# Reordering the opening of a fused linear-attention and SwiGLU kernel: half of nd, x and q transposes, and the k phi of the next batch

## Chip, cores, metric

One core of a Trainium2 chip. The metric is the device time of one execution in microseconds (us), median of a kernel's runs. All timed runs named here are in the fast state, but for the single run of e4, whose state is unknown. A ratio is the mean time of one kernel's fast runs over the mean of the other's in the same rounds, so it is not quite the ratio of the medians quoted beside it.

## The reference, cut to what matters

```python
# q, k, v: 8 batches x 8 heads x 576 tokens x 64
def phi(x, c, s):                       # c, s: cos and sin of the token's place
    r = np.maximum(x, 0.0)
    return np.concatenate([r * c, r * s], axis=-1)
kv  = np.einsum('bhsf,bhsd->bhfd', phi(k), v);   z = np.sum(phi(k), axis=2)
num = np.einsum('bhsf,bhfd->bhsd', phi(q), kv)
den = np.einsum('bhsf,bhf->bhs', phi(q), z)[..., None] + 1e-06
x   = num / den                         # tokens x 512
xn  = x / sqrt(mean(x * x) + 1e-6) * rms_g
g   = xn @ w_gate;  val = xn @ w_val    # 512 -> 1536
out = (silu(g) * val) @ w_out           # 1536 -> 512
```

Of the kernel before, what the change touches and what calls it, by code (L numbers as in the profile page):

```python
# [23 lines left out]
def kernel(  # L24
# [30 lines left out]
    psA = ps.tile([P, 2, 512], FP32, name="psA")  # L55
# [8 lines left out]
    V, A, G = nc.vector, nc.scalar, nc.gpsimd  # L64
# [160 lines left out]
    def q_phi(eng, b, c, part):  # L225
        o = slice(0, D) if part == 0 else slice(D, F)
        f = cos_of if part == 0 else sin_of
        if (b, c) not in qp_tiles:
            qp_tiles[(b, c)] = four.tile(
                [P, H if c < 4 else 4, F], BF16, name="qp", tag="qp" if c < 4 else "qpt"  # L230
            )
        src = view4(raw[("q", b)], c) if c < 4 else raw[("qt", b)][:, :, :]
        phi(eng, qp_tiles[(b, c)][:, :, o], src, f(c))
# [15 lines left out]
    def q_tr_pe(b, c, bank):  # L249
        t = qp_tiles[(b, c)]  # L250
        dst = bank.bitcast(BF16).rearrange("p (h s) -> p h s", s=P)
        for h in range(H if c < 4 else 4):
            nc.tensor.transpose(dst[:, h, :], t[:, h, :], ident[:, :])  # L253

    def q_tr_evac(eng, b, c, bank, heads=(0, 8)):
        h0, h1 = heads if c < 4 else (0, 4)
        dst = bank.bitcast(BF16).rearrange("p (h s) -> p h s", s=P)
        copy(eng, q_dst(b, c)[:, h0:h1, :], dst[:, h0:h1, :])

    def copy(eng, o, i):  # L260
        if eng is nc.scalar:
            nc.scalar.copy(out=o, in_=i)  # L262
        else:
            eng.tensor_copy(out=o, in_=i)  # L264
# [10 lines left out]
    def kvz_mm(b, banks, rs=(0, 4)):  # L275

        for r in range(*rs):
            for j in range(NJ):
                for c in range(2):
                    lo = 64 * c  # L280
                    nc.tensor.matmul(  # L281
                        banks[c][:, r * E : (r + 1) * E],
                        lhsT=kp_main[b][lo : lo + 64, j, r, :],
                        rhs=vvm[b % 2][lo : lo + 64, r, j, :],
                        start=(j == 0), stop=(j == NJ - 1),
                    )
# [4 lines left out]
    def kvz_copy(eng, b, c, bank, rs=(0, 4)):  # L291
        if (b, c) not in kvzs:
            kvzs[(b, c)] = three.tile([P, 4 * E], BF16, name="kvzs", tag=f"kvzs{c}")
        lo, hi = rs[0] * E, rs[1] * E
        copy(eng, kvzs[(b, c)][:, lo:hi], bank[:, lo:hi])
# [7 lines left out]
    def nd_pe(b, j, pst):  # L303

        o = headview(pst)
        for h in range(H):
            g, i = h // 4, h % 4
            if j < 4:
                nc.tensor.matmul(  # L309
                    o[:, g, i, :], lhsT=qpT[(b, 0)][:, h, j * P : (j + 1) * P],  # L310
                    rhs=kvz_of(b, h), start=True, stop=True,
                )
            else:
                for bb in (b - 1, b):
                    lo = 64 * (bb % 2)
                    nc.tensor.matmul(
                        o[lo : lo + 64, g, i, :],
                        lhsT=qpT[(bb, 1)][:, i, 64 * g : 64 * g + 64],
                        rhs=kvz_of(bb, h), start=True, stop=True,
                    )  # L320

    def nd_half(b, j, g, bank):
        o = bank[:, 0 : 4 * E].rearrange("p (h e) -> p h e", e=E)
        for i in range(4):
            nc.tensor.matmul(
                o[:, i, :], lhsT=qpT[(b, 0)][:, 4 * g + i, j * P : (j + 1) * P],
                rhs=kvz_of(b, 4 * g + i), start=True, stop=True,
            )
# [11 lines left out]
    def nd_post_half(b, j, g, bank):  # L340
        o = bank[:, 0 : 4 * E].rearrange("p (h e) -> p h e", e=E)
        xt = x_tile(b, j)
        rec = four.tile([P, 2, 4], FP32, name="rec", tag="rec")
        nc.vector.tensor_scalar(
            out=rec[:, g, :], in0=o[:, :, D], scalar1=1e-6, scalar2=None, op0=ALU.add
        )
        nc.vector.reciprocal(out=rec[:, g, :], in_=rec[:, g, :])
        nc.vector.tensor_tensor(
            out=xt[:, g * DM // 2 : (g + 1) * DM // 2].rearrange("p (h d) -> p h d", d=D),
            in0=o[:, :, 0:D],  # L350
            in1=rec[:, g, :].unsqueeze(2).to_broadcast([P, 4, D]),
            op=ALU.mult,
        )

    def nd_post(b, j, pst):
        o = headview(pst)
        xt = x_tile(b, j)
        rec = four.tile([P, 2, 4], FP32, name="rec", tag="rec")
        nc.vector.tensor_scalar(
            out=rec[:, :, :], in0=o[:, :, :, D], scalar1=1e-6, scalar2=None, op0=ALU.add  # L360
        )
        nc.vector.reciprocal(out=rec[:, :, :], in_=rec[:, :, :])
        nc.vector.tensor_tensor(  # L363
            out=xt[:, 0:DM].rearrange("p (b h d) -> p b h d", b=2, d=D),
            in0=o[:, :, :, 0:D],
            in1=rec[:, :, :].unsqueeze(3).to_broadcast([P, 2, 4, D]),
            op=ALU.mult,
        )

    def x_sq(b, j):  # L370
        xt = x_of[(b, j)]
        scr = one.tile([P, DM + 1], BF16, name="scr", tag="scr")
        ms = four.tile([P, 1], FP32, name="ms", tag="ms")
        nc.scalar.activation(  # L374
            out=scr[:, :], in_=xt[:, 0 : DM + 1], func=AF.Square,
            scale=1.0 / math.sqrt(DM), accum_out=ms[:, :],
        )
        rs = four.tile([P, 1], FP32, name="rs", tag="rs")
        nc.gpsimd.tensor_tensor(out=rs[:, :], in0=ms[:, :], in1=mhalf[:, :], op=ALU.pow)  # L379
        rs_of[(b, j)] = rs  # L380
# [82 lines left out]
    def filler(n, bank):  # L463
        for _ in range(n):
            nc.tensor.matmul(bank, lhsT=warm[:, 0:P], rhs=warm[:, :], start=True, stop=True)
# [60 lines left out]
    v_cast(V, 0, 3, 4)  # L526
    kvz_mm(0, high_banks, (2, 3))
    filler(1, idle)
    kvz_mm(0, high_banks, (3, 4))
    kvz_copy(A, 0, 0, high_banks[0], HIGH)  # L530
    kvz_copy(A, 0, 1, high_banks[1], HIGH)
    q_tr_evac(V, 0, 1, psO[0][:, :])
    nd_half(0, 0, 0, psV[0])
    nd_post_half(0, 0, 0, psV[0])
    filler(1, idle)
    nd_half(0, 0, 1, psO[1])
    nd_post_half(0, 0, 1, psO[1])
    copy(A, gb[:, :], psG[0][:, :])
    nd_pe(0, 1, psA)
    q_phi(A, 0, 2, 1)  # L540
    x_sq(0, 0)
    nd_post(0, 1, psA)
    filler(8, psV[1][:, :])
    q_phi(A, 0, 3, 1)
    q_phi(V, 0, 2, 0)
    x_sq(0, 1)
    gval_slice(768, 1152)
    gval_slice(1152, 1536)
    q_tr_pe(0, 2, psO[0][:, :])
    q_tr_evac(A, 0, 2, psO[0][:, :])  # L550
    x_norm(0, 0)
    q_phi(V, 0, 3, 0)
    filler(1, psV[1][:, :])

    def open_ffn(pair, steps, c0, c1, base=0, parts=(0, 1)):

        x = xnT[0]
        for i, n in enumerate(steps):
            for a in parts:
                w = (wg, wv)[a]  # L560
                bank = pairs[pair][a]
                lo = base + 256 * i + c0 % 256
                for t in range(NDT):
                    nc.tensor.matmul(  # L564
                        bank[:, lo : lo + c1 - c0],
                        lhsT=w[:, t, n * P : (n + 1) * P], rhs=x[:, t, c0:c1],
                        start=(t == 0), stop=(t == NDT - 1),
                    )
# [13 lines left out]

    x_tr_pe(0, 0, psG[1][:, :])
    x_tr_evac(V, 0, 0, psG[1][:, :])
    q_tr_pe(0, 3, psO[1][:, :])
    x_norm(0, 1)
    open_ffn(0, (0, 1), 0, 128)
    x_tr_pe(0, 1, psV[1][:, :])
    q_tr_evac(A, 0, 3, psO[1][:, :])
    x_tr_evac(V, 0, 1, psV[1][:, :])  # L590
    nd_pe(0, 2, psA)
    nd_post(0, 2, psA)
    x_sq(0, 2)
    wo_load(0)
    filler(1, psG[1][:, :])
    open_ffn(0, (0, 1), 128, 256)
    nd_pe(0, 3, psA)
    nd_post(0, 3, psA)
    open_ffn(1, (2, 3), 0, 256)
    open_h(0, 0, 0)  # L600
    x_norm(0, 2)
    x_sq(0, 3)
    open_ffn(2, (4, 5), 0, 256, parts=(0,))
    x_tr_pe(0, 2, psA[:, 0, :])
    x_tr_evac(A, 0, 2, psA[:, 0, :])
    open_h(1, 2, 0)
    x_norm(0, 3)
    open_ffn(0, (0, 1), 256, 384)
    open_ffn(2, (4, 5), 0, 256, parts=(1,))
    x_tr_pe(0, 3, psA[:, 1, :])  # L610
    x_tr_evac(A, 0, 3, psA[:, 1, :])
    open_h(2, 4, 0)
    open_ffn(0, (0, 1), 384, 512)
    open_h(0, 0, 1)
# [33 lines left out]


    for j in range(NJ):  # L650
        at(0, 9 + j // 5, "post", k_phi, V, 1, j, 0)
        at(0, 9 + j // 5, "post", k_phi, A, 1, j, 1)
    for c in range(2):
        at(0, 11, "post", q_phi, V, 1, c, 0)
        at(0, 11, "post", q_phi, A, 1, c, 1)


    for nb in range(2, B):
# [203 lines left out]
```

## The kernel before: what the change touches

Nine blocks of 512 tokens run one after another. Block 0 has its attention at the very start (the *opening*); all later attention work hides beside the matrix products of earlier blocks (PE is busy 263.4 of the last 268.9 us). The names: `phi` is a relu times cos and sin (see the reference); `psA`, `psG`, `psO`, `psV` are tiles in PSUM, which TensorE writes and ScalarE or VectorE copy out; `kvz` is k-z-v (phi(k) times v with a column of ones); `nd` is numerator and denominator, phi(q) times kvz, for one group of 128 tokens; `x_sq` and `x_norm` make the normed x; `x_tr_pe` transposes it on TensorE into PSUM, and `x_tr_evac` copies it to `xnT`, which the gate and value products (`open_ffn`) read. `q_phi`, `q_tr_pe` and `q_tr_evac` do the same for q. `filler` is a product of zeros that keeps TensorE going. The traces show TensorE and ScalarE keeping to program order: in the kernel before TensorE stood 0.67 us until 24.79 for the copy of x2, and the products into `psO` that stand behind it and do not need x2 came at 25.68; in e4 ScalarE stood 3.48 us for k, and the SiLU behind it came at 38.09.

```python
    kvz_mm(0, high_banks, (2, 3))
    filler(1, idle)
    kvz_mm(0, high_banks, (3, 4))
    kvz_copy(A, 0, 0, high_banks[0], HIGH)
    kvz_copy(A, 0, 1, high_banks[1], HIGH)
    q_tr_evac(V, 0, 1, psO[0][:, :])
    nd_half(0, 0, 0, psV[0])
    nd_post_half(0, 0, 0, psV[0])
    filler(1, idle)
    nd_half(0, 0, 1, psO[1])
    nd_post_half(0, 0, 1, psO[1])
    copy(A, gb[:, :], psG[0][:, :])
    nd_pe(0, 1, psA)
    q_phi(A, 0, 2, 1)
    x_sq(0, 0)
    nd_post(0, 1, psA)
    filler(8, psV[1][:, :])
    q_phi(A, 0, 3, 1)
    q_phi(V, 0, 2, 0)
    x_sq(0, 1)
    gval_slice(768, 1152)
    gval_slice(1152, 1536)
    q_tr_pe(0, 2, psO[0][:, :])
    q_tr_evac(A, 0, 2, psO[0][:, :])
    x_norm(0, 0)
    q_phi(V, 0, 3, 0)
    filler(1, psV[1][:, :])
    ...
    x_tr_pe(0, 0, psG[1][:, :])
    x_tr_evac(V, 0, 0, psG[1][:, :])
    q_tr_pe(0, 3, psO[1][:, :])
    x_norm(0, 1)
    open_ffn(0, (0, 1), 0, 128)
    x_tr_pe(0, 1, psV[1][:, :])
    q_tr_evac(A, 0, 3, psO[1][:, :])
    x_tr_evac(V, 0, 1, psV[1][:, :])
    nd_pe(0, 2, psA)
    nd_post(0, 2, psA)
    x_sq(0, 2)
    wo_load(0)
    filler(1, psG[1][:, :])
    open_ffn(0, (0, 1), 128, 256)
    nd_pe(0, 3, psA)
    nd_post(0, 3, psA)
    open_ffn(1, (2, 3), 0, 256)
    open_h(0, 0, 0)
    x_norm(0, 2)
    x_sq(0, 3)
    open_ffn(2, (4, 5), 0, 256, parts=(0,))
    x_tr_pe(0, 2, psA[:, 0, :])
    x_tr_evac(A, 0, 2, psA[:, 0, :])
    open_h(1, 2, 0)
    x_norm(0, 3)
    open_ffn(0, (0, 1), 256, 384)
    open_ffn(2, (4, 5), 0, 256, parts=(1,))
    x_tr_pe(0, 3, psA[:, 1, :])
    x_tr_evac(A, 0, 3, psA[:, 1, :])
    open_h(2, 4, 0)
    open_ffn(0, (0, 1), 384, 512)
    ...
    for j in range(NJ):                  # k and q phi of batch 1, at steps 9 to 11 of block 0
        at(0, 9 + j // 5, "post", k_phi, V, 1, j, 0)
        at(0, 9 + j // 5, "post", k_phi, A, 1, j, 1)
    for c in range(2):
        at(0, 11, "post", q_phi, V, 1, c, 0)
        at(0, 11, "post", q_phi, A, 1, c, 1)
```

Steps 0 to 5 of block 0 are done in the opening, in halves and quarters of the 512 tokens; steps 6 to 11 (`gval_step`) are full width: four 128x512 products for the gate, four for the value, then a SiLU on ScalarE and a product hT on VectorE. What is attached to a step as "post" is issued behind those.

## Time and profile before

| | before |
|---|---|
| time, median of the first 3 runs | 330.49 us (330.29 to 331.8) |
| span of the profiled run | 328.9 us |
| TensorE (PE) busy | 316.5 us, 96% |
| PE busy in the last 268.9 us | 263.4 us |
| PE idle in the first 60 us | 6.9 us |

The lines themselves stand in the prediction. How to read them: a row of the order in time gives start, duration, engine, source line, what is written from what, and in brackets how long the engine stood idle before it and what ended that. A line number can be a helper's: L411 is a transpose of x, L253 one of q, L564 the products of the opening (L561 in the kernel after), L425 the full-width gate and value products, L445 the output product, L281 the k-z-v, L208 the phi on ScalarE. The idle time in brackets is counted from the modelled end of the row before, not from its start. A DMA share over 1 is as the view gives it; I read it as full. The durations 1.01, 0.58 and 0.42 us that the prediction uses are those of the trace for a copy out of PSUM: 1024 columns on ScalarE (L262, qpT), 512 on ScalarE (L262, xnT), 512 on VectorE (L264, xnT). From 27 to 31 us the weights' queue has a DMA share of 1.24, the queue of k, q and v 0.04.

### The profile page before, as it was taken

Reading aid. Unit: us, or ns where it says so; the run is one execution under the profiler, and the core shown is the slowest. Engines: PE = TensorE matmul, PEld = TensorE weight load, DVE = VectorE, ACT = ScalarE, POOL = GpSimd, SP = SyncE. Lnnn points to the kernel's source line nnn. Section 1 sums busy time; section 2 is a strip of 40 time slices with the busy share of each in tenths; the row PEclk is TensorE's granted clock in tenths of the full one; section 3 lists DMA queues with packets and bytes.
Section 4 is the critical chain, followed back from the end, with each engine's and each line's share of the span. In section 5 each row is a group of like instructions: output and inputs, shape, how many; then the busy total and the mean of one; then the engine's idle time right before and its main releaser. Section 6 shows DMA issues by size and latency. Waiting matters only on the chain.

```text
span 328.9 us, 6376 instructions
## 1 busy us (share of the span) xinstructions
PE 316.5 (96%) x2392; PEld 161.2 (49%) x2428; DVE 186.6 (57%) x412; ACT 175.3 (53%) x364; POOL 32.1 (10%) x67
## 2 busy tenths in 40 slices
PE   6898989999999999999999999999999999999995
PEld 2577455654445444544454445444554444444443
DVE  5974586777764776577357745773567234204410
ACT  6754575885556547645665566446654243223321
POOL 1660102001100110011001100110001000000000
PEclk9999999999999999999999999999999999999999
DMA  7999999859968966996688568967631410030014
GB/s 260 228 196 237 352 193 352 259 132 194 258 169 204 192 181 173 246 196 150 209 198 190 164 188 209 186 170 213 137 66 32 125 36 0 2 118 10 0 34 96
DMA packets 80193, 53.91 MB, mean 164 GB/s; under 512 B 51361, under 2 KB 67489, under 8 KB 80162
## 3 DMA queue, kind: packets, MB, share of 16 engines
q1 hardware_dynamic: 73120, 48.64, 57.1%
q0 software_dynamic: 6880, 4.72, 10.1%
q8 instruction: 19, 0.31, 0.4%
q10 hardware_dynamic: 162, 0.13, 0.2%
q14 instruction: 12, 0.10, 0.1%
HBM read 37.75 MB, written 9.44 MB: 143 GB/s over the span
## 4 chain that ended last, share of the span: by engine, by line
PE 88%; ACT 4%; DMA 2%; DVE 2%; issue 2%; SPq 1%; POOL 0%
PE psC L445 26%; PE psG L425 25%; PE psV L425 25%; PE psA L281 3%; DMA rv<-in_v_dram 2%; PE psA L309 2%; ACT kpm L208 2%; PE psG L445 1%; PE psG L564 1%; PE psV L564 1%; PE psO L564 1%; ACT sg L434 1%; SPq L79 1%; PE psV L253 1%; ACT qp L208 1%
## 5 line engine op out<-in xcount | busy, mean ns | idle before, releaser
L440 DVE TENSOR_TENSOR hT<-psV,sg 128x512 bf16<-128x512 f32 x102 | 70.3, 689 | 97.1 <-PE psV L425 73.1
L434 ACT ACTIVATE sg<-psG 128x512 f32<-128x512 f32 x102 | 60.5, 593 | 66.1 <-PE psG L425 63.5
L425 PE MATMUL psV<-xnT,wv 128*128 128x512 bf16 (+1 forms) x365 | 92.1, 374 | 0.4
L425 PE MATMUL psG<-xnT,wg 128*128 128x512 bf16 (+1 forms) x352 | 90.9, 374 | 0.7
L445 PE MATMUL psC<-wo,hT 128*128 128x512 bf16 x382 | 88.2, 379 | 0.7
L425 PEld LDWEIGHTS <-wv 128*128 128x128 bf16 x416 | 40.7, 98 | 47.4
L445 PEld LDWEIGHTS <-hT 128*128 128x128 bf16 x420 | 40.2, 98 | 46.4
L425 PEld LDWEIGHTS <-wg 128*128 128x128 bf16 x416 | 38.6, 98 | 41.3 <-DVE xnT L264 0.4
L262 ACT COPY osb<-psC 128x512 f32<-128x512 f32 (+1 forms) x33 | 19.1, 578 | 40.1 <-PE psC L445 39.4
L379 POOL TENSOR_TENSOR rs<-ms,mhalf 128x1 f32<-128x1 f32 x36 | 20.0, 555 | 203.2 <-ACT scr L374 203.2
L374 ACT ACTIVATE scr<-xt 128x513 bf16<-128x513 f32 x36 | 22.9, 635 | 24.4 <-DVE xt L363 23.9
L386 DVE SCALAR_TENSOR_TENSOR xn<-xt,rs,gb 128x512 bf16<-128x512 f32 x36 | 26.8, 745 | 14.0 <-POOL rs L379 13.9
L208 ACT ACTIVATE kpm<-rk,tab 128x256 bf16<-128x256 f32 (+1 forms) x78 | 31.7, 477 | 1.8 <-DMA rk<-in_k_dram 1.8
L363 DVE TENSOR_TENSOR xt<-psA,rec 128x512 f32<-128x512 f32 x35 | 24.2, 691 | 1.2
L210 DVE TENSOR_SCALAR kpm<-rk,tab 128x256 bf16<-128x256 f32 (+1 forms) x84 | 22.7, 336 | 2.3 <-DMA rk<-in_k_dram 2.3
L208 ACT ACTIVATE qp<-rq,tab 128x512 bf16<-128x512 f32 x31 | 21.7, 713 | 0.0
L210 DVE TENSOR_SCALAR qp<-rq,tab 128x512 bf16<-128x512 f32 x33 | 15.2, 477 | 0.0
L309 PEld LDWEIGHTS <-qpT 128*128 128x128 bf16 x248 | 11.6, 98 | 6.5 <-issue 0.3
L309 PE MATMUL psA<-kvzs,qpT 128*128 128x65 bf16 x248 | 12.6, 193 | 0.1
L425 PE MATMUL psG<-xnt_tail,wg 128*128 128x512 bf16 x48 | 12.3, 379 | 0.1
L425 PE MATMUL psV<-xnt_tail,wv 128*128 128x512 bf16 x47 | 12.1, 379 | 0.0
L281 PEld LDWEIGHTS <-kpm 64*128 64x128 bf16 x576 | 10.0, 95 | 3.7 <-issue 2.9
(90 smaller groups left out, 166.9 us busy)
## 6 DMA issues: line engine op xcount, KB each, us to landing
out_dram<-osb SPq DMA_DIRECT2D x32, 256.0 KB, 2.6
rv<-in_v_dram SPq DMA_DIRECT2D x22, 288.0 KB, 3.3
rk<-in_k_dram SPq DMA_DIRECT2D x20, 288.0 KB, 3.5
rq<-in_q_dram SPq DMA_DIRECT2D x20, 256.0 KB, 3.2
rk<-in_k_dram SPq DMA_DIRECT2D x2, 1152.0 KB
rq<-in_q_dram SPq DMA_DIRECT2D x2, 1024.0 KB, 10.8
rv<-in_v_dram SPq DMA_DIRECT2D x3, 576.0 KB, 9.5
wo<-in_moe_w_out_dram POOLq DMA_DIRECT2D x4, 384.0 KB, 6.9
```

The lines of the kernel that those rows point to most:

```text
L208: nc.scalar.activation(out=out_ap, in_=in_ap, func=AF.Relu, scale=scale)
L210: eng.tensor_scalar(out=out_ap, in0=in_ap, scalar1=scale, scalar2=0.0, op0=ALU.mult, op1=ALU.max)
L281: nc.tensor.matmul(banks[c][:, r * E : (r + 1) * E], lhsT=kp_main[b][lo : lo + 64, j, r, :], rhs=vvm[b % 2][lo : lo + 64, r, j, :], start= ...
L309: nc.tensor.matmul(o[:, g, i, :], lhsT=qpT[(b, 0)][:, h, j * P : (j + 1) * P], rhs=kvz_of(b, h), start=True, stop=True,)
L363: nc.vector.tensor_tensor(out=xt[:, 0:DM].rearrange("p (b h d) -> p b h d", b=2, d=D), in0=o[:, :, :, 0:D], in1=rec[:, :, :].unsqueeze(3). ...
L374: nc.scalar.activation(out=scr[:, :], in_=xt[:, 0 : DM + 1], func=AF.Square, scale=1.0 / math.sqrt(DM), accum_out=ms[:, :],)
L379: nc.gpsimd.tensor_tensor(out=rs[:, :], in0=ms[:, :], in1=mhalf[:, :], op=ALU.pow)
L386: nc.vector.scalar_tensor_tensor(out=xn[:, :], in0=x_of[(b, j)][:, 0:DM], scalar=rs_of[(b, j)][:, :], in1=gb[:, :], op0=ALU.mult, op1=ALU. ...
L425: nc.tensor.matmul(pst[bank][:, cols[0] : cols[1]], lhsT=w[:, t, n * P : (n + 1) * P], rhs=x[:, t, cols[0] : cols[1]], start=(t == 0), sto ...
L434: nc.scalar.activation(out=sg[:, :], in_=psG[bank][:, :], func=AF.Silu)
L440: nc.vector.tensor_tensor(out=hTs[blk][:, n, :], in0=psV[bank][:, :], in1=sg[:, :], op=ALU.mult)
L445: nc.tensor.matmul(bank, lhsT=hTs[blk][:, n, j * P : (j + 1) * P], rhs=wo[:, n, :], start=(n == 0), stop=(n == NNT - 1),)
```

## The change

Its intent: let the first x start sooner (half of nd ahead of the last k-z-v head, and VectorE relieved of one copy); put products between each transpose of x and the products that need it; put the q transposes behind those of x; and spread the phi of batch 1 over steps 8 to 10 so that ScalarE is done when TensorE needs its banks and q.

```diff
--- before.py
+++ after.py
@@ -526,31 +526,28 @@
     v_cast(V, 0, 3, 4)
     kvz_mm(0, high_banks, (2, 3))
     filler(1, idle)
+    nd_half(0, 0, 0, psV[0])
+    nd_post_half(0, 0, 0, psV[0])
     kvz_mm(0, high_banks, (3, 4))
+    q_tr_evac(A, 0, 1, psO[0][:, :], (0, 4))
     kvz_copy(A, 0, 0, high_banks[0], HIGH)
     kvz_copy(A, 0, 1, high_banks[1], HIGH)
-    q_tr_evac(V, 0, 1, psO[0][:, :])
-    nd_half(0, 0, 0, psV[0])
-    nd_post_half(0, 0, 0, psV[0])
     filler(1, idle)
     nd_half(0, 0, 1, psO[1])
     nd_post_half(0, 0, 1, psO[1])
+    q_tr_evac(A, 0, 1, psO[0][:, :], (4, 8))
     copy(A, gb[:, :], psG[0][:, :])
+    x_sq(0, 0)
     nd_pe(0, 1, psA)
+    nd_post(0, 1, psA)
     q_phi(A, 0, 2, 1)
-    x_sq(0, 0)
-    nd_post(0, 1, psA)
-    filler(8, psV[1][:, :])
-    q_phi(A, 0, 3, 1)
-    q_phi(V, 0, 2, 0)
     x_sq(0, 1)
     gval_slice(768, 1152)
     gval_slice(1152, 1536)
-    q_tr_pe(0, 2, psO[0][:, :])
-    q_tr_evac(A, 0, 2, psO[0][:, :])
+    filler(9, psV[1][:, :])
     x_norm(0, 0)
-    q_phi(V, 0, 3, 0)
-    filler(1, psV[1][:, :])
+    q_phi(V, 0, 2, 0)
+    q_phi(A, 0, 3, 1)
 
     def open_ffn(pair, steps, c0, c1, base=0, parts=(0, 1)):
 
@@ -582,33 +579,37 @@
 
     x_tr_pe(0, 0, psG[1][:, :])
     x_tr_evac(V, 0, 0, psG[1][:, :])
-    q_tr_pe(0, 3, psO[1][:, :])
+    q_tr_pe(0, 2, psO[0][:, :])
+    q_tr_evac(A, 0, 2, psO[0][:, :])
+    q_phi(V, 0, 3, 0)
     x_norm(0, 1)
     open_ffn(0, (0, 1), 0, 128)
     x_tr_pe(0, 1, psV[1][:, :])
-    q_tr_evac(A, 0, 3, psO[1][:, :])
     x_tr_evac(V, 0, 1, psV[1][:, :])
     nd_pe(0, 2, psA)
     nd_post(0, 2, psA)
+    q_tr_pe(0, 3, psO[1][:, :])
+    q_tr_evac(A, 0, 3, psO[1][:, :])
     x_sq(0, 2)
     wo_load(0)
-    filler(1, psG[1][:, :])
     open_ffn(0, (0, 1), 128, 256)
+    open_ffn(1, (2, 3), 0, 256, parts=(0,))
     nd_pe(0, 3, psA)
     nd_post(0, 3, psA)
-    open_ffn(1, (2, 3), 0, 256)
+    x_norm(0, 2)
+    open_ffn(1, (2, 3), 0, 256, parts=(1,))
     open_h(0, 0, 0)
-    x_norm(0, 2)
     x_sq(0, 3)
     open_ffn(2, (4, 5), 0, 256, parts=(0,))
     x_tr_pe(0, 2, psA[:, 0, :])
     x_tr_evac(A, 0, 2, psA[:, 0, :])
+    x_norm(0, 3)
+    open_ffn(2, (4, 5), 0, 256, parts=(1,))
+    open_ffn(0, (0, 1), 256, 384, parts=(0,))
+    x_tr_pe(0, 3, psA[:, 1, :])
+    x_tr_evac(V, 0, 3, psA[:, 1, :])
+    open_ffn(0, (0, 1), 256, 384, parts=(1,))
     open_h(1, 2, 0)
-    x_norm(0, 3)
-    open_ffn(0, (0, 1), 256, 384)
-    open_ffn(2, (4, 5), 0, 256, parts=(1,))
-    x_tr_pe(0, 3, psA[:, 1, :])
-    x_tr_evac(A, 0, 3, psA[:, 1, :])
     open_h(2, 4, 0)
     open_ffn(0, (0, 1), 384, 512)
     open_h(0, 0, 1)
@@ -648,11 +649,11 @@
 
 
     for j in range(NJ):
-        at(0, 9 + j // 5, "post", k_phi, V, 1, j, 0)
-        at(0, 9 + j // 5, "post", k_phi, A, 1, j, 1)
+        at(0, 8 + j // 4, "post", k_phi, V, 1, j, 0)
+        at(0, 8 + j // 4, "post", k_phi, A, 1, j, 1)
     for c in range(2):
-        at(0, 11, "post", q_phi, V, 1, c, 0)
-        at(0, 11, "post", q_phi, A, 1, c, 1)
+        at(0, 10 + c, "post", q_phi, V, 1, c, 0)
+        at(0, 10 + c, "post", q_phi, A, 1, c, 1)
 
 
     for nb in range(2, B):
```

## Prediction

> **What bounds the kernel now.** I read the page first, then the busy time by stretch, then the order in time of TensorE, ScalarE, VectorE and the DMA issues for the first 60 us. From the page, busy time, and the stretches (us, PE, PEld, DVE, ACT, POOL, clock, DMA share, GB/s):
>
> ```profile
> PE 316.5 (96%) x2392; PEld 161.2 (49%) x2428; DVE 186.6 (57%) x412; ACT 175.3 (53%) x364; POOL 32.1 (10%) x67
> ```
>
> ```profile
> 13.00:18.01 5.01, 4.13 (x46) 2.43 (x46) 4.45 (x15) 4.47 (x10) 3.67 (x6) 1.00 1.28 154
> 18.01:32.13 14.12, 12.72 (x160) 11.05 (x158) 7.71 (x15) 6.54 (x13) 4.46 (x7) 1.00 1.32 213
> 32.13:42.49 10.36, 10.31 (x49) 4.70 (x48) 5.95 (x11) 6.27 (x14) 2.34 (x3) 1.00 1.03 318
> 42.49:60.00 17.51, 16.12 (x198) 9.77 (x200) 13.00 (x32) 11.25 (x22) 2.21 (x4) 1.00 1.06 278
> 60.00:328.90 268.90, 263.39 (x1840) 128.53 (x1868) 146.03 (x309) 138.31 (x285) 15.34 (x28) 1.00 0.59 143
> ```
>
> PE sets the end, in program order. After 60 us it starts a block every 0.86 us for four 128x512 products and its waits are too short to list, so a microsecond won before 60 us should arrive whole at the end. Before that, the waits that matter are these (start, duration, idle before it):
>
> ```profile
> 13.79 1.89 PE L465 MATMUL psV<-warm 128*128 128x512 bf16 x8
> 16.34 0.61 PE L253 MATMUL psO<-ident,qp 128*128 128x128 bf16 x8 [0.66 <-DVE qp L210]
> 18.01 0.39 PE L564 MATMUL psG<-xnT,wg 128*128 128x128 bf16 x4
> 23.72 0.40 PE L411 MATMUL psA<-ident,xn 128*128 128x128 bf16 x4
> 24.79 0.38 PE L564 MATMUL psG<-xnT,wg 128*128 128x128 bf16 x4 [0.67 <-ACT xnT L262]
> 26.68 0.40 PE L411 MATMUL psA<-ident,xn 128*128 128x128 bf16 x4
> 27.75 0.38 PE L564 MATMUL psG<-xnT,wg 128*128 128x128 bf16 x4 [0.67 <-ACT xnT L262]
> 43.57 0.38 PE L445 MATMUL psG<-wo,hT 128*128 128x512 bf16 x1 [0.26 <-ACT sg L434]
> 44.78 0.61 PE L253 MATMUL psV<-ident,qp 128*128 128x128 bf16 x8 [0.84 <-ACT qp L208]
> ```
>
> Twice a transpose of x (L411) is followed at once by the products that read it, so PE stands through the copy out of PSUM: 23.72 to 24.79 and 26.68 to 27.75, where 0.22 of each 1.07 us is work. At 43.57 and 44.78 it waits for ScalarE, which is still at the k and q phi of batch 1. The fillers at 13.79 cover the chain to the first x and win nothing by being shorter.
>
> [...]
> - [...] a block of four 128x128 products lasts 0.39 us, the next starts 0.22 us after it, and work behind a waiting block does not pass it.
> - [...] The trace has 1.01, 0.58 and 0.42, so I use these.
> - [...] mean DMA share is 1.28 and 1.32 in the opening, and the weights land one after another (24.8, 27.1, 28.9, 30.9 us)[...]
> - [...] So when k of batch 1 lands must be worked out (below).
>
> **The change, part by part.** I walk the after order with the durations above; a hand-over between engines costs 0.03 to 0.11 us as in the trace, a VectorE row occupies its engine some 0.07 and a ScalarE row 0.09 us less than its duration.
>
> (1) First x. The second q transpose's copy leaves VectorE (0.68 us) for ScalarE in two halves of 0.58 (0.16 us more in all, in ScalarE's wait for the last k-z-v head and after it). Half of nd and its division go ahead of that head: xt's first half is ready at 13.3, not 14.0. The second half still waits for the kvz copies (13.41), PE runs it at 13.29 as before, and its division starts at 13.74 instead of 13.95. So square, power and norm come 0.2 us sooner: norm at 16.03, not 16.27; transpose of x0 at 16.83 to 17.05; copy to 17.68. The q transpose for token group 2 now follows it (17.28 to 17.73) and covers that copy; first products at 17.74, **0.27 us sooner** than 18.01. PE does the same other work: a filler more (nine) and two single ones fewer.
>
> (2) x1 to x3. Products 17.74 to 18.62. x1's norm comes after VectorE's last q phi and ends at 18.75 (before 18.59); transpose 18.80; nd of group 2 19.02 to 19.26; q transpose 3 to 19.71; products of x1's columns (xnT at 19.65) 19.71 to 20.60, first two 256-wide blocks to 21.48, nd of group 3 to 21.72, three more and one pair to 23.47. VectorE divides group 3 from 21.92 to 23.04, norms x2 to 23.72; transpose of x2 at 23.77 to 23.99. That is no sooner than before (23.72), because the q transpose of 0.45 us now lies in here. But behind it: two psO products (0.87 us) to 24.86, while ScalarE copies x2 out, 24.21 to 24.79; the gate half of the next columns to 25.30; x3 (square 23.14, power to 24.5, norm to 25.27) transposes 25.32 to 25.54; its copy, on VectorE, is 25.75 to 26.17, beside the value half (to 25.98). So the last columns start at 26.23 instead of 27.75: both stalls of 0.67 go, and **the opening gains 1.5 us**. The full-width steps then begin at 30.6 instead of 32.1. Weights are no new wait: the latest, for columns 512 to 768, landed at 23.1 and is wanted at 24.0.
>
> (3) k phi. The slots are 1.73 us, so step 8's SiLU ends near 35.6. If k is there: 4 x 0.42, SiLU 0.48, 4 x 0.42, SiLU 0.48, one k and one q phi (0.42 + 0.62), SiLU 0.60 = 6.0 us, to 41.6. PE reaches the second psG of the output at 30.6 + 6 x 1.73 + 0.65 = 41.6 and does not wait; q phi for its transposes is there too. That takes the 0.26 + 0.84 us and about 0.2 of refilling away: at most **1.3 us**.
>
> But is k there? Landings counted from the issues: q of batch 1, queued behind k, at 27.65 + 11.3 = 38.95; v's halves at 40.7 and 42.2. The halves, 0.59 MB each, took 1.75 and 1.5 us; at that rate q's 1.05 MB take 2.8, so by estimate **k lands near 36.1**. Its issue hangs on a weight landing at 27.1[...]. ScalarE then stands 0.5 us, the last SiLU ends at 42.1, and PE waits 0.5 us at 41.6: the gain is 1.3 - 0.5 = 0.8 to 0.9 us.
>
> Then kvz of batch 1 starts at 45.1 instead of 47.49 (v's cast, ScalarE's last before it, ends at 45.0). wo's second part lands at 44.5, so no wait there. **Sum: 1.5 + 0.9 = 2.4 us**, 330.49 - 2.4 = **328.1 us**.
>
> **Rivals.**
> (a) k in time. If k's packets have the queue to themselves sooner and it lands by 35.6, the whole 1.3 counts: 327.6. For it: in 33 to 39 us the DMAs move 370 to 390 GB/s. Against: until 30.9 the weights hold most of them, at 200 GB/s.
> (b) k late. If k, q and v advance side by side rather than in turn, k lands after 37, ScalarE is held at step 8, and later SiLUs and the q phi slip with it: PE waits 1.4 us or more at the output, and the change keeps only the opening: 329.0 or a little more. ScalarE's wait for DMA at the first k phi would show it.
> (c) VectorE or ScalarE becomes the bound of the opening. x2's chain has no slack: x1's norm is 0.16 later, nd of group 3 behind two products. Each 0.2 us added (a power op took 0.75 instead of 0.56 once) goes straight to the transpose of x2 or x3. With two such, the opening gains 1.0 and the time is 328.6.
> (d) Hidden anyway: k2, gated on wo's second part, would have to arrive too late for its phi. k2 is issued at 46.5 and q2 behind it lands at 57.5; its phi moves from 61.5 to 59.1. I hold this for unlikely.
>
> **Range and chances.** (a) and (b) span 327.6 to 329.0; (c) adds up to half a microsecond, and three runs of before already lie 1.5 us apart (330.29 to 331.8), so I take 327.2 to 329.4. Faster by 2% would need 6.6 us; all waits of PE before 60 us together (60 less 53.1 busy) are 6.9, much of it before the data is there: 1%. Slower by 2% would need a wait in the steady state that no step makes: 1%. Within 2%: 98%.
>
> **What would show it.** Right: the two waits for xnT on ScalarE at L564 are gone or under 0.2 us; the x2 transpose stands near 23.8, the last opening columns near 26.2, the first full-width step near 30.6; ScalarE waits about 0.5 us for k at its first k phi of batch 1 near 35.6; PE's wait at the second output bank is near 0.5 and the one for q phi gone; kvz of batch 1 near 45.1; from there on the two traces run parallel, and PE's busy time is the same within 0.5 us. Wrong: a transpose of x2 later than 24.3, a k landing after 37, a new wait for a weight DMA in the opening, or a shift at 60 us that is not the shift at the end.

## The result, and the profile after

The kernel after took 328.19 us median of 4 runs (327.96 to 328.54), the kernel before 331.05 beside it; ratio 0.9914, 95% interval 0.9885 to 0.9944, all runs fast. A repetition later gave 0.9923 (0.9902 to 0.9944). The predicted 328.1 was within 0.1 us of the median, and the ratio is within the 2% that the prediction gave 98%. The single terms were not all right, and they erred in opposite directions.

The page of the profile after, busy time; then the stretches cut at the same events as in the prediction (first products of the opening, first full-width step, first output product, 60 us, end; columns as there):

```profile
PE 318.9 (98%) x2427; PEld 161.3 (49%) x2427; DVE 186.3 (57%) x412; ACT 175.7 (54%) x365; POOL 31.9 (10%) x67
```

```profile
18.37:31.43 13.06, 12.74 (x167) 11.40 (x165) 8.50 (x17) 6.86 (x13) 4.26 (x7) 1.00 1.34 202
31.43:41.79 10.36, 10.36 (x50) 4.68 (x48) 6.59 (x16) 7.40 (x17) 1.86 (x3) 1.00 1.02 343
41.79:60.00 18.21, 18.00 (x221) 11.29 (x220) 13.49 (x31) 11.71 (x23) 2.77 (x5) 1.00 1.09 279
60.00:326.70 266.70, 262.94 (x1850) 127.03 (x1847) 144.58 (x305) 136.75 (x282) 15.33 (x28) 1.00 0.60 144
```

The stretch from the first products to the full-width steps went from 14.12 to 13.06 us, with 0.32 us of it idle on PE instead of 1.40. The order in time of PE after, the rows that answer to those of before:

```profile
17.44 0.40 PE L411 MATMUL psG<-ident,xn 128*128 128x128 bf16 x4 [0.71 <-DVE xn L386]
17.92 0.61 PE L253 MATMUL psO<-ident,qp 128*128 128x128 bf16 x8
18.37 0.39 PE L561 MATMUL psG<-xnT,wg 128*128 128x128 bf16 x4
...
23.27 1.04 PE L561 MATMUL psO<-xnT,wg 128*128 128x256 bf16 x8
24.45 0.40 PE L411 MATMUL psA<-ident,xn 128*128 128x128 bf16 x4
24.68 1.04 PE L561 MATMUL psO<-xnT,wv 128*128 128x256 bf16 x8
25.56 0.61 PE L561 MATMUL psG<-xnT,wg 128*128 128x128 bf16 x8
26.07 0.40 PE L411 MATMUL psA<-ident,xn 128*128 128x128 bf16 x4
26.30 0.61 PE L561 MATMUL psV<-xnT,wv 128*128 128x128 bf16 x8
27.05 0.38 PE L561 MATMUL psG<-xnT,wg 128*128 128x128 bf16 x4
...
42.22 0.59 PE L445 MATMUL psG<-wo,hT 128*128 128x512 bf16 x2
42.66 0.61 PE L253 MATMUL psV<-ident,qp 128*128 128x128 bf16 x8
```

Behind each transpose of x (24.45, 26.07) stand products that do not need it, and the two idle times of 0.67 are gone. What is left is smaller: the eight products at 23.27 are issued by 24.14 (0.87 us), and the transpose of x2 comes 0.3 us later, when its norm is done; the eight at 26.30 are issued by 26.74, and the last columns start 0.31 us later, behind the copy of x3. These two carry no bracket, since the modelled end of the row before hides most of each. At 42.22 and 42.66 PE no longer waits for ScalarE. And ScalarE at the first k phi of batch 1:

```profile
35.95 0.60 ACT L434 ACTIVATE sg<-psG 128x512 f32<-128x512 f32 x1 [1.13 <-PE psG L425]
36.47 1.70 ACT L208 ACTIVATE kpm<-rk,tab 128x256 bf16<-128x256 f32 x4
```

There is no bracket on the second row: the wait for k of 0.5 us that I had predicted did not come.

**Four stretches.** To compare traces whose start differs by how soon the first v lands, I cut each at four events seen in the order in time: **H** from the start to the fourth (last) k-z-v head, the second group of rows that write psA at L281; **D** from there to the first full-width step; **B** from there to the k-z-v of batch 1; **C** from there to the end. The rows of the cuts, with the transpose of x0 of the kernel before; before, then after:

```profile
12.47 0.46 PE L281 MATMUL psA<-vvm,kpm 64*128 64x65 bf16 x18 [0.44 <-DVE vvm L264]
17.08 0.40 PE L411 MATMUL psG<-ident,xn 128*128 128x128 bf16 x4
32.13 1.03 PE L425 MATMUL psG<-xnT,wg 128*128 128x512 bf16 x3
47.49 1.33 PE L281 MATMUL psA<-vvm,kpm 64*128 64x65 bf16 x72
```

```profile
13.01 0.47 PE L281 MATMUL psA<-vvm,kpm 64*128 64x65 bf16 x18
31.43 1.03 PE L425 MATMUL psG<-xnT,wg 128*128 128x512 bf16 x4
45.37 1.33 PE L281 MATMUL psA<-vvm,kpm 64*128 64x65 bf16 x72
```

| | H | D | B | C | span |
|---|---|---|---|---|---|
| before | 12.47 | 19.66 | 15.36 | 281.41 | 328.9 |
| after | 13.01 | 18.42 | 13.94 | 281.33 | 326.7 |
| difference | +0.54 | -1.24 | -1.42 | -0.08 | -2.2 |

H is not the change's: ScalarE's cast of the first v began at 10.60 instead of 10.06 because v landed later in that run (ScalarE's wait for it there is 0.82 us, before 0.32); the same kernel, run again (e11), had an H of 12.13. Without it the traces differ by 2.74 us, and 0.86% of 331.05 is 2.85. C does not move: what is won before the k-z-v of batch 1 arrives whole at the end.

In the expectations below, written before this table, **A** runs from the *third* head instead of the fourth. It proved a poor mark: the third head can start late and the fourth not, as it waits for v's last piece (0.44 us for its cast at 12.47): from one to the other took 0.91 us in the kernel before and 0.71 in e1, where that code is the same. Read D.

### The profile page after: what moved, and what is told of

It is laid out like the page before. It is cut to its first block, busy times and chain, and to the rows that moved or that the text cites. A ratio compares the mean times of both kernels' runs of the same rounds, so it can differ in the third digit from the quotient of the medians.

```text
span 326.7 us, 6408 instructions
## 1 busy us (share of the span) xinstructions
PE 318.9 (98%) x2427; PEld 161.3 (49%) x2427; DVE 186.3 (57%) x412; ACT 175.7 (54%) x365; POOL 31.9 (10%) x67
## 4 chain that ended last, share of the span: by engine, by line
PE 91%; DMA 3%; DVE 2%; ACT 2%; issue 1%; SPq 0%; POOL 0%; DVEq 0%
PE psG L425 26%; PE psC L445 26%; PE psV L425 26%; PE psA L281 3%; DMA rv<-in_v_dram 3%; PE psA L309 2%; PE psG L445 1%; PE psG L561 1%; PE psO L561 1%; PE psV L561 1%; ACT kpm L208 1%; PE psV L253 1%; ACT sg L434 0%; PE psA L316 0%; DVE xn L386 0%
## 5 line engine op out<-in xcount | busy, mean ns | idle before, releaser
L425 PE MATMUL psG<-xnT,wg 128*128 128x512 bf16 (+1 forms) x368 | 92.9, 375 | 0.1
L425 PE MATMUL psV<-xnT,wv 128*128 128x512 bf16 (+1 forms) x368 | 92.7, 374 | 0.0
L445 PE MATMUL psC<-wo,hT 128*128 128x512 bf16 x396 | 89.6, 379 | 0.0
L425 PEld LDWEIGHTS <-wv 128*128 128x128 bf16 x416 | 40.6, 98 | 47.4
L425 PEld LDWEIGHTS <-wg 128*128 128x128 bf16 x416 | 38.5, 98 | 41.3 <-DVE xnT L264 0.4
L425 PE MATMUL psV<-xnt_tail,wv 128*128 128x512 bf16 x48 | 12.3, 379 | 0.0
L425 PE MATMUL psG<-xnt_tail,wg 128*128 128x512 bf16 x48 | 12.3, 379 | 0.0
L281 PEld LDWEIGHTS <-kpm 64*128 64x128 bf16 x576 | 9.9, 95 | 3.8 <-issue 2.7
```

The costliest lines, as they stand in the source:

```text
L281: nc.tensor.matmul(banks[c][:, r * E : (r + 1) * E], lhsT=kp_main[b][lo : lo + 64, j, r, :], rhs=vvm[b % 2][lo : lo + 64, r, j, :], start= ...
L425: nc.tensor.matmul(pst[bank][:, cols[0] : cols[1]], lhsT=w[:, t, n * P : (n + 1) * P], rhs=x[:, t, cols[0] : cols[1]], start=(t == 0), sto ...
L445: nc.tensor.matmul(bank, lhsT=hTs[blk][:, n, j * P : (j + 1) * P], rhs=wo[:, n, :], start=(n == 0), stop=(n == NNT - 1),)
```

## Experiments

All of them gave correct results. Their stretches in one table; e4 was one look and has no ratio.

| run | H | D | B | C | median us | ratio to before, 95% |
|---|---|---|---|---|---|---|
| e1 k phi only | 13.45 | 19.66 | 13.94 | 281.35 | 329.82 | 0.9962 (0.9937 to 0.9988) |
| e2 opening only | 12.43 | 18.41 | 15.36 | 281.40 | 329.48 | 0.9961 (0.9932 to 0.9991) |
| e3 head only | 12.65 | 19.49 | 15.35 | 281.41 | 330.71 | 0.9982 (0.9960 to 1.0004) |
| e4 k phi at 6 to 8 | 12.93 | 18.41 | 16.49 | 281.37 | 330.97 | (one run) |
| e5 no lead | 12.76 | 19.32 | 13.93 | 281.39 | 329.46 | 0.9952 (0.9900 to 1.0004) |
| e6 q ahead | 12.44 | 18.19 | 13.94 | 281.33 | 327.89 | 0.9892 (0.9857 to 0.9927) |
| e7 late k | 12.57 | 18.43 | 14.52 | 281.38 | 328.92 | 0.9922 (0.9887 to 0.9958) |
| e8 q2, x1, nd3 | 12.50 | 17.80 | 14.34 | 281.36 | 328.41 | 0.9908 (0.9867 to 0.9949) |
| e9 = e8, k early | 13.11 | 17.80 | 13.94 | 281.35 | 327.85 | 0.9911 (0.9892 to 0.9930) |
| e10 = e8, k between | 12.47 | 17.81 | 13.94 | 281.38 | 327.42 | 0.9901 (0.9882 to 0.9920) |
| e11 after again | 12.13 | 18.42 | 13.94 | 281.41 | 328.04 | 0.9923 (0.9902 to 0.9944) |
| e12 no fillers | 13.01 | 19.59 | 13.94 | 281.36 | 329.52 | 0.9959 (0.9940 to 0.9978) |

The stretches repeat to 0.01 or 0.02 us wherever their code is the same, while H wanders over 1.3 us. So a difference of 0.2 us in a stretch can be read from one trace, though the interval of total times is up to 3.4 us wide (e5).

### e1: the k phi alone

```diff
 (in the kernel before)
-        at(0, 9 + j // 5, "post", k_phi, V, 1, j, 0)      # and for A
+        at(0, 8 + j // 4, "post", k_phi, V, 1, j, 0)
-        at(0, 11, "post", q_phi, V, 1, c, 0)
+        at(0, 10 + c, "post", q_phi, V, 1, c, 0)
```

> The kernel before with only the k and q phi of batch 1 a step earlier. Three stretches: A from the third k-z-v head (first write of psA by L281) to the first full-width step, B from there to the k-z-v of batch 1, C from there to the end; before A 20.57, B 15.36, C 281.4; after A 19.32, B 13.94, C 281.3. Theory (the two parts are independent and k is in time): A stays 20.6, B falls to 13.9 to 14.0, no wait for q phi at the output; time about 1.4 us under the kernel before. Rival (k lands only just in time for the later, unshortened opening; the gain is k's landing, not ScalarE's order): ScalarE waits for DMA at its first k phi and B stays above 14.5.

B fell to 13.94 with no wait for the q phi at the output; time 1.26 us less (0.38% of 331.6). D is that of before. As expected, no wait for k: here step 8 comes later.

### e2: the opening alone

```diff
 (in the kernel after)
-        at(0, 8 + j // 4, "post", k_phi, V, 1, j, 0)      # all four lines of e1 back
+        at(0, 9 + j // 5, "post", k_phi, V, 1, j, 0)
```

> The kernel after with the k and q phi back in their old steps. Theory: A 19.3, B 15.3 to 15.4 with the two waits for ScalarE of 0.26 and 0.84 back; time 1.2 to 1.3 us under the kernel before, so that this gain and that of k phi alone add up to the whole. Rival (the old waits were for transfers at fixed times, so an earlier opening only lengthens them): B 16 or more, and the gains do not add up.

D is that of after, B that of before to 0.01 us, with its waits of 0.26 and 0.84 back; 0.39%, or 1.29 us. The two gains add up to 2.55 us; the whole measured 2.85 and, repeated, 2.55 (0.77% of 330.7). The parts are independent, and the rival of transfers at fixed times falls.

### e3: the head alone

```diff
 (in the kernel before)
+    nd_half(0, 0, 0, psV[0]); nd_post_half(0, 0, 0, psV[0])
     kvz_mm(0, high_banks, (3, 4))
+    q_tr_evac(A, 0, 1, psO[0][:, :], (0, 4))
     kvz_copy(A, 0, 0, high_banks[0], HIGH); kvz_copy(A, 0, 1, high_banks[1], HIGH)
-    q_tr_evac(V, 0, 1, psO[0][:, :])
-    nd_half(0, 0, 0, psV[0]); nd_post_half(0, 0, 0, psV[0])
 ...
+    q_tr_evac(A, 0, 1, psO[0][:, :], (4, 8))
     copy(A, gb[:, :], psG[0][:, :])
+    x_sq(0, 0)
     nd_pe(0, 1, psA)
     q_phi(A, 0, 2, 1)
-    x_sq(0, 0)
```

> The kernel before with only the head of the change: first half of nd ahead of the last k-z-v head, the second q transpose copied by ScalarE in two halves, the first square ahead of a q phi. Theory: the first x is normed 0.2 us sooner after the third k-z-v head starts (4.71 before, 4.52 after), and all of the opening follows by that: A 20.3 to 20.4, B unchanged 15.36, time 0.2 us less, which the total alone cannot show. Rival (q transposes and the phi between them hold the chain, so the sooner x is lost): A stays 20.5 to 20.6.

The transpose of x0 comes 4.42 us after the fourth head, 4.61 before, 4.43 in the kernel after; D falls by 0.17. The total time (interval 0.9960 to 1.0004) shows nothing, as it could not. So the head is worth 0.17 to 0.19 us of the opening's 1.24.

### e4: the k phi two steps earlier still, to see k land

```diff
 (in the kernel after)
-        at(0, 8 + j // 4, "post", k_phi, V, 1, j, 0)      # and for A
+        at(0, 6 + j // 4, "post", k_phi, V, 1, j, 0)
```

> The kernel after with k phi of batch 1 two steps earlier still (steps 6 to 8), to see when k lands: at step 6 it cannot be there. My estimate on record was 36.1 us in the trace of before, where its DMA was issued at 27.1, that is 9.0 after the issue; the trace after bounds it to 8.8 or less. Theory (k goes ahead of q and v and has most of the queue once the weights are in): ScalarE waits for DMA at the first k phi, and that wait ends 7 to 8.5 us after the issue of k. If it ends over 8.5 the bound was just met; under 7, the weights hold the queue less than I took. The time should rise by 0.5 us or more, as the later SiLUs queue behind the wait.

k's row of the DMA issues starts in e4 at 27.41 and lasts 0.38 us, while ScalarE waits for k until 36.48: the row is the issue, not the movement, and for this transfer the profile gives no landing (for the q and v behind it, it does). A consumer put too early makes it visible. ScalarE in e4:

```profile
32.41 0.60 ACT L434 ACTIVATE sg<-psG 128x512 f32<-128x512 f32 x1 [0.70 <-PE psG L425]
36.48 1.70 ACT L208 ACTIVATE kpm<-rk,tab 128x256 bf16<-128x256 f32 x4 [3.48 <-DMA rk<-in_k_dram]
```

k was issued at 27.41 and is used at 36.48, 9.07 us later. My estimate on record was 9.0; the figure of 7 to 8.5 that I wrote for this run was the worse one. The landing differs a little from run to run: in the kernel after ScalarE took k without a wait 8.88 us after the issue. B rose by 2.55 us, since the SiLUs queue behind the wait.

### e5: the lead of the x transposes taken away

```diff
 (in the kernel after)
     open_ffn(2, (4, 5), 0, 256, parts=(0,))
+    open_ffn(2, (4, 5), 0, 256, parts=(1,))
     x_tr_pe(0, 2, psA[:, 0, :]); x_tr_evac(A, 0, 2, psA[:, 0, :])
     x_norm(0, 3)
-    open_ffn(2, (4, 5), 0, 256, parts=(1,))
     open_ffn(0, (0, 1), 256, 384, parts=(0,))
+    open_ffn(0, (0, 1), 256, 384, parts=(1,))
     x_tr_pe(0, 3, psA[:, 1, :]); x_tr_evac(V, 0, 3, psA[:, 1, :])
-    open_ffn(0, (0, 1), 256, 384, parts=(1,))
```

> The kernel after with the lead of the x transposes taken away and nothing else: the psO products stand ahead of the transpose of x2, and the transpose of x3 behind both halves of the columns before it, so the products that read each follow at once. Theory: PE again waits through both copies (about 0.7 us for x2, 0.5 for x3, whose copy is on VectorE); but the wait of 0.3 us for the norm of x2 is filled and so is that for the first-half copy, so A grows by 0.6 to 0.8 us only, from 19.3 to about 20.0, not by 2 x 0.67 us. Rival (the whole gain of the opening is those two waits): A back at 20.5 or more.

PE in e5, order in time:

```profile
24.77 0.39 PE L411 MATMUL psA<-ident,xn 128*128 128x128 bf16 x4
25.83 0.61 PE L561 MATMUL psG<-xnT,wg 128*128 128x128 bf16 x8 [0.67 <-ACT xnT L262]
26.27 0.61 PE L561 MATMUL psV<-xnT,wv 128*128 128x128 bf16 x8
26.72 0.39 PE L411 MATMUL psA<-ident,xn 128*128 128x128 bf16 x4
27.69 0.38 PE L561 MATMUL psG<-xnT,wg 128*128 128x128 bf16 x4 [0.58 <-DVE xnT L264]
```

Both waits are back, 0.67 behind ScalarE's copy and 0.58 behind VectorE's shorter one, and D is 0.90 us longer (0.85 by A, where I expected 0.6 to 0.8). So the lead is worth 0.90 of the 1.24. That is not what the brackets add up to (1.25 here, 1.34 before), and the account closes only from start to start: from a transpose to the next products pass 1.06 and 0.97 us here, of which a block takes 0.22, so the two stalls cost 0.84 and 0.75. With the lead PE stands 0.31 us for the norm of x2, 0.07 before the transpose of x3 and 0.31 for the copy of x3, and 1.59 less 0.69 is 0.90. Head (e3) and lead leave 0.16 of the 1.24; 0.10 of that is the copy of x3 on VectorE (its stall is 0.85 in the kernel before, 0.75 here), the rest no run assigns.

### e6: the q transposes ahead again

```diff
 (in the kernel after)
     q_phi(A, 0, 2, 1)
+    q_phi(V, 0, 2, 0)
 ...
     filler(9, psV[1][:, :])
+    q_tr_pe(0, 2, psO[0][:, :])
     x_norm(0, 0)
-    q_phi(V, 0, 2, 0)
     q_phi(A, 0, 3, 1)
+    q_tr_evac(A, 0, 2, psO[0][:, :]); q_phi(V, 0, 3, 0)
     x_tr_pe(0, 0, psG[1][:, :]); x_tr_evac(V, 0, 0, psG[1][:, :])
-    q_tr_pe(0, 2, psO[0][:, :]); q_tr_evac(A, 0, 2, psO[0][:, :]); q_phi(V, 0, 3, 0)
+    q_tr_pe(0, 3, psO[1][:, :]); q_tr_evac(A, 0, 3, psO[1][:, :])
     x_norm(0, 1)
 ...
     nd_post(0, 2, psA)
-    q_tr_pe(0, 3, psO[1][:, :]); q_tr_evac(A, 0, 3, psO[1][:, :])
```

> The kernel after with the q transposes where they were: the one of group 2 ahead of the transpose of x0 in the time of the fillers, the one of group 3 in the copy of x0. Theory (the step of my prediction that put 0.45 us of q transpose into the busy part): the q transpose of group 2 is then done where PE waits for the first x anyway, the transpose of x2 comes 0.4 to 0.5 us sooner, and A falls from 19.3 to about 18.9: moving q behind x cost, it did not gain. Rival (q transposes delay the first x, as the change takes it): the transpose of x0 comes later than 5.33 us after the third k-z-v head starts, and A is 19.4 or more.

The first x is no later (its transpose 4.42 us after the fourth head, as in after), so the rival falls; D is 0.23 us *shorter* than after. Moving q behind x cost time. The size was half of what I wrote: with the third q transpose gone from behind the transpose of x1, nothing covers that copy, and PE shows a new wait for it:

```profile
18.69 0.39 PE L411 MATMUL psV<-ident,xn 128*128 128x128 bf16 x4
18.91 0.41 PE L309 MATMUL psA<-kvzs,qpT 128*128 128x65 bf16 x8
19.59 0.38 PE L564 MATMUL psG<-xnT,wg 128*128 128x128 bf16 x4 [0.27 <-DVE xnT L264]
```

### e7: k issued late

```diff
 (in the kernel after)
-    tc.add_manual_dep(d.ins, weight_dmas[7].ins.name, SYNC_DEP, reason="after the weights")
+    tc.add_manual_dep(d.ins, weight_dmas[9].ins.name, SYNC_DEP, reason="after the weights")
```

> The kernel after with k of batch 1 issued only after the last weight has landed (some 3.8 us later), q and v behind it too. This sizes my rival (b). Theory: k lands 1.5 to 3 us later than in the kernel after, since the weights it yields to are out of the way; ScalarE waits for it at its first k phi of step 8, the SiLUs behind slip by as much, and PE waits at the output: B grows by about the length of ScalarE's wait less 0.1 us of slack, A and C stay. If B does not grow with a wait on ScalarE of over 0.5 us, rival (b) was no danger.

k was issued at 31.16 and landed at 36.78: 5.6 us later, not 9. From the fourth head that is an issue 4.1 us later than in e4 and a landing only 0.66 us later, less than the 1.5 to 3 expected. ScalarE waited 0.68 us for it, and B grew by 0.58: the wait, less 0.1 us of slack. So a late k, the danger of rival (b), costs time, here nearly one to one.

```profile
36.78 1.70 ACT L208 ACTIVATE kpm<-rk,tab 128x256 bf16<-128x256 f32 x4 [0.68 <-DMA rk<-in_k_dram]
```

### e8: an opening shorter still

```diff
 (in the kernel after; as in e6 up to the transpose of x0, but q_phi(V, 0, 3, 0) stays below)
     x_tr_pe(0, 0, psG[1][:, :]); x_tr_evac(V, 0, 0, psG[1][:, :])
-    q_tr_pe(0, 2, psO[0][:, :]); q_tr_evac(A, 0, 2, psO[0][:, :])
-    q_phi(V, 0, 3, 0)
+    filler(2, psV[1][:, :])
     x_norm(0, 1)
+    q_phi(V, 0, 3, 0)
 ...
-    open_ffn(1, (2, 3), 0, 256, parts=(0,))
+    open_ffn(1, (2,), 0, 256, parts=(0,))
     nd_pe(0, 3, psA); nd_post(0, 3, psA)
     x_norm(0, 2)
+    open_ffn(1, (3,), 0, 256, base=256, parts=(0,))
```

> A version meant to beat both: q transpose 2 in the filler time, two fillers in the copy of x0, the norm of x1 ahead of VectorE's last q phi, and nd of group 3 after one 256-wide block instead of two. Worked out on the trace after: transpose of x1 at 7.15 us after the third k-z-v head starts (7.35 after), the transpose of x2 at 11.8 (12.34), last opening columns at 14.1 (14.94), A about 18.5 instead of 19.3; then step 8 comes sooner and k may be waited for, by up to 0.5 us. Time 0.5 to 0.8 us under the kernel after, 3 us under before. If A falls only to 18.9 as with q ahead alone, the earlier nd of group 3 is lost on VectorE.

D fell to 17.80, 0.62 less than after, with the transposes of x1 and x2 at 7.10 and 11.77 us from the third head (7.15 and 11.8 expected). But B rose by 0.40, so that D and B together are only 0.22 shorter than after, where I expected 0.5 to 0.8, and the total is not clear of the kernel after. The predicted wait for k came as soon as step 8 came sooner:

```profile
34.82 0.60 ACT L434 ACTIVATE sg<-psG 128x512 f32<-128x512 f32 x1 [1.13 <-PE psG L425]
35.91 1.31 ACT L208 ACTIVATE kpm<-rk,tab 128x256 bf16<-128x256 f32 x3 [0.49 <-DMA rk<-in_k_dram]
```

k was issued at 26.96, so it took 8.95 us here.

### e9 and e10: the same with k issued earlier, and e11: after again

```diff
 (in e8)
-    tc.add_manual_dep(d.ins, weight_dmas[7].ins.name, SYNC_DEP, reason="after the weights")
+    tc.add_manual_dep(d.ins, weight_dmas[5].ins.name, SYNC_DEP, reason="after the weights")   # e9; [6] in e10
```

> The version of e8_q2_x1_nd3 with k of batch 1 released by the sixth weight transfer (columns 512 to 768) instead of the eighth, so its issue is some 3.5 us earlier, at about 23.5. With the late k (issued 3.75 us later it landed only 0.7 us later), [...] the earlier issue should bring it 0.5 to 1.5 us earlier, not 3.5; that clears the wait of 0.49 us, and B goes from 14.34 back to 13.9, A stays 18.7: span 325.6, about 1.0 us under the kernel after from the same start. Rival: k takes its bandwidth from the last four weight transfers, and PE waits for one of them at the first full-width steps (none waits now); then A or B grows by that wait and nothing is won.

> The same with k released by the seventh weight transfer, about 2 us earlier than in e8_q2_x1_nd3. Theory: half of the effect, k 0.3 to 0.8 us earlier, wait of ScalarE for k 0 to 0.2 us, B 13.9 to 14.1. If the sixth gives a wait for weights and this none, this is the better version.

> The kernel after, unaltered, beside the two on one chip: B 13.94 and C 281.3 as before, A 19.3; from the fourth k-z-v head (second group of writes of psA) to the first full-width step 18.42 as in the first trace. The two new versions should be 0.6 to 1.1 us under it.

In both the wait for k is gone and B is 13.94 again. Counted from the fourth head, k was issued 4.36 and 2.74 us earlier than in e8, and ScalarE takes it 0.6 us earlier without a wait; how much earlier it landed, these runs only bound. In e9 a weight load for L425 waits 0.2 us for a weight transfer, without cost to the stretch; in e10 nothing waits. By the mark set beforehand e10 is the better one, but the times do not tell them apart (from the fourth head to the end 313.09 and 313.13 us). From the fourth head to the end e10 takes 17.81 + 13.94 + 281.38 = 313.13 us, the kernel after beside it 18.42 + 13.94 + 281.41 = 313.77: 0.64 us less. The medians, 327.42 and 328.04, say the same, but their intervals overlap (0.9882 to 0.9920, and 0.9902 to 0.9944): shown in the trace, not beyond doubt in the totals.

### e12: the kernel after without its nine fillers

```diff
-    filler(9, psV[1][:, :])
```

> The kernel after without its nine fillers ahead of the first transpose of x. On record: they cover the chain to the first x and win or cost nothing by their length. Theory: PE stands some 2.8 us there, transpose of x0 4.43 us after the fourth k-z-v head starts as now, and A is the same within 0.1 us if the granted clock stays at 1.00; rival: the clock falls after the pause, products of 128x128 behind it take longer than 0.22 us a block, and A grows by 1 us or more.

The transpose of x0 comes at 4.42, so the fillers hold nothing up. But without them PE pauses for 2.64 us, and D grows by 1.17:

```profile
17.43 0.61 PE L411 MATMUL psG<-ident,xn 128*128 128x128 bf16 x4 [2.64 <-DVE xn L386]
```

Stretches of e12 (columns as before; the clock is the third number from the right):

```profile
13.00:17.00 4.00, 1.63 (x33) 0.98 (x31) 2.88 (x10) 3.30 (x10) 3.15 (x5) 1.00 1.20 139
17.00:21.00 4.00, 3.57 (x37) 3.46 (x38) 2.25 (x5) 1.78 (x4) 3.52 (x5) 0.57 1.39 184
21.00:24.00 3.00, 3.00 (x53) 2.87 (x50) 1.59 (x6) 2.12 (x4) 0.53 (x2) 1.00 1.38 201
```

The granted clock is 0.57 from 17 to 21 us, behind the pause, 1.00 from 13 to 17 and again from 21 to 24, and a block of four 128x128 products starts every 0.43 us instead of 0.22. The length of one pause does not account for it alone: in e1 the clock was 0.50 from 10 to 12 us, though PE's longest pause since its first product was, by the brackets, 0.88 us (6.14 to 7.02), while in the kernel before a pause of 1.50 us at the same place was followed by no fall (clock 1.00 from 8 to 13 us). By an estimate from the clock of each microsecond (0.53, 0.50, 0.50, 0.76 from 9 us in e1; 0.73, 0.50, 0.50, 0.57 from 17 us in e12) it was at half for 3.4 us both times, 9.1 to 12.5 in e1 and 17.5 to 20.9 in e12. What else decides it these runs do not show. My remark on record that the fillers "win nothing by being shorter" is right as far as it goes; that they are worth 1.17 us it did not say.

## Why the prediction was right, and where it was not

The places of the prediction, counted from the fourth k-z-v head (its own time less 12.47), against the trace after (less 13.01):

| | predicted | measured |
|---|---|---|
| transpose of x0 | 4.36 | 4.43 |
| transpose of x1 | 6.33 | 6.45 |
| transpose of x2 | 11.30 | 11.44 |
| transpose of x3 | 12.85 | 13.06 |
| last columns of the opening | 13.76 | 14.04 |
| first full-width step | 18.1 | 18.42 |
| end of the SiLU of step 8 | 23.1 | 23.46 |
| k of batch 1 landed | 23.6 | 23.41 (e8), 23.55 (e4) |
| k-z-v of batch 1 | 32.6 | 32.36 |

**The opening (predicted 1.5, measured 1.24).** The mechanism was right in every part: the head brings 0.17 to 0.19 us (0.2 predicted; e3), the two waits of 0.67 go, x2 itself comes no sooner (here even 0.19 later than before), the lead is what pays (e5: 0.90), and the q transpose costs in its new place (e6). The term was mis-sized by 0.26 us. The table shows how: each link of the chain from x0 to the last columns is a few hundredths longer than I had it, and the chain has no slack to absorb that. This is rival (c) at half its size. (One count in the text is wrong, not its sum: the "three more and one pair" between nd of group 3 and 23.47 are, by the time given and by the trace after (22.40 and 23.27), two pairs of blocks.)

**The k phi (predicted 0.8 to 0.9, measured 1.42).** The failed step is "ScalarE then stands 0.5 us". The landing of k was estimated well: 9.0 us after its issue, and e4 and e8 measured 9.07 and 8.95. What was off is the other side of the race: the SiLU of step 8 ended 0.3 us later than I had it, almost all of it because the opening gained less. ScalarE came when k did, and did not wait. So the two misses are mostly one: an opening 0.3 us too fast in my working made 0.3 of a wait of 0.5 us where there was none; the other 0.2 is that k had landed by 23.46 after the head, where I had 23.63. e8 closes the argument: with the opening 0.62 us shorter, the wait of 0.49 us appears. The upper bound I gave, 1.3, was 0.1 low. A product row lasts 0.38 us, but without a wait the next starts 0.22 after it; from start to start the two waits cost 0.43 (42.92 to 43.57) and 0.99 (43.57 to 44.78), together the 1.42, while the brackets say 0.26 and 0.84.

**k's issue.** The working takes it as unmoved. From the fourth head that holds (14.61 before, 14.58 after), but the whole row of transfers starts behind the first v (the first weight is issued at 10.34 before and 10.88 after, when GpSimd's wait for v ends), so k moves with H from run to run (issued at 27.08 before, 27.59 after, 26.54 in e11). It is not a fixed time. Issued 2.74 us earlier, k came at least 0.59 us earlier (e10 against e8); whether a weight issued earlier lands earlier no run tests.

**The signs.** Three of the signs on record mislead as they were written. The transpose of x2 stands at 24.45, past the 24.3 that was to mean "wrong"; 0.54 us of that is H. PE's busy time was to stay within 0.5 us and rose from 316.5 to 318.9, but the change takes away one filler and the page counts 2427 matmuls instead of 2392: the trace of before lacks some records, so its busy sum is not to be compared to a microsecond. And the wait for k, with PE's wait of 0.5 at the output, did not come.

**The rivals.** (a) is what came about, by a late SiLU and not by an early k. (b) did not happen; that a late k costs time e7 shows (0.68 of wait, 0.58 of time), but the 1.4 us I gave it was not run. (d) was rightly dismissed: C is the same in all fourteen traces within 0.1 us.

**Range and chances.** The measured 328.19 lies in 327.2 to 329.4. The two errors, 0.26 too much and about 0.55 too little, partly cancelled; the agreement with 328.1 is better than the working deserves. And the kernel before rose from 330.49 to 331.05 with one more run: H alone spreads over 1.3 us among the traces, about as much as either part of the change is worth.

What stays open: which of the edits in e8 gives how much of its 0.62 us (e6 shows only that q transposes kept ahead bring 0.23), and why H differs by over a microsecond between runs. Part of it is v's landing; in e1 it was the clock as well, which was granted at 0.50 from 10 to 12 us, so that the first eight q transposes took 1.06 us instead of 0.62. The four runs of e1 go with their mean granted clock: 329.40 us at 1.000, 329.45 at 0.999, 330.19 at 0.995, 330.64 at 0.992.

## What to carry to other kernels

Where a transpose is followed at once by its consumer, put independent products between them, but size the gain by what else the engine will then wait for: taking away two stalls of 0.84 and 0.75 us was worth 0.90 together. Measure a stall from start to start of the rows around it; the bracket leaves out what a row without a wait would have overlapped (0.67 for a stall of 0.84, e5). When a consumer is moved earlier, work out the landing of its input and the arrival of the engine from the same event; the result turns on their difference, and a chain that is a few hundredths too fast at each link is enough to put a wait in or take it out. And before work is moved out of the way of a critical chain, look whether it stood in a wait, where it cost nothing: the q transposes behind x cost 0.23 us (e6).
